# Row layout of tanh in a speech joint network: TensorE transposes with a PSUM copy, or SBUF-to-SBUF DMA transposes

## The chip, the cores and the metric

The kernel runs on one core of a Trainium2 chip. The metric is the device time of one execution in microseconds. A profiled execution also has a span, from its first to its last recorded instruction. The core has five engines with instruction queues of their own: TensorE (PE in the profile; PEld is its weight load), VectorE (DVE), ScalarE (ACT), GpSimd (POOL) and SyncE (SP), which here only issues DMAs.

## The reference

The forward pass is a small convolutional encoder and a joint network, and the reference returns its output and the gradients of all seven inputs. Cut to what matters:

```python
# x (2, 16000, 256), g (2, 8, 256); w1, w2 (3, 256, 256); w_f, w_g, w_o (256, 256), all bfloat16
h  = gelu(conv(x, w1))[:, ::2, :]            # three taps, then every second row: 8000 rows
f  = gelu(conv(h, w2))[:, ::2, :]            # 4000 rows
fe = einsum("btd,de->bte", f, w_f)
ge = einsum("bud,de->bue", g, w_g)
j  = tanh(fe[:, :, None, :] + ge[:, None, :, :])   # (2, 4000, 8, 256)
out = einsum("btud,dv->btuv", j, w_o)
# returned: out and the gradients of x, w1, w2, g, w_f, w_g, w_o for a given grad_out (2, 4000, 8, 256)
```

The product that the change touches is the gradient of w_o ("gwo"): the sum over b, t and u of j[b,t,u,d] * grad_out[b,t,u,v]. It contracts over t, so TensorE needs j with t on the partitions ("row layout"). The other uses of j, the output product and the derivative 1 - j*j, need or have d on the partitions ("column layout").

## The kernel before, in words

The 4000 rows of each of the two batches are cut into nine chunks: seven of 512 rows, one of 256 and one of 160, 18 chunks in all. For a chunk there are three stages, written as generators: stage_a (lines 243 to 293) computes the encoder up to FE and the row layouts HRo, HRe and FR; stage_j (331 to 401) is the joint network with its gradients; stage_de (438 to 552) is the rest of the backward pass, down to the gradients of x and of the encoder's weights. The main loop (626 to 649) runs them staggered: in iteration k it takes stage_j of chunk k, stage_a of chunk k+1 and stage_de of chunk k-1 in turns, in 16 steps. The scheduler of the language places the instructions on the engines' queues from this order and from the dependencies; on each queue they then run in order.

In stage_j the eight values of u are taken as four pairs (`up`), each of four steps. A step is one (j, dt): j is which u of the pair, dt which half of the 256 columns. Each step holds:

- gj (line 349): the product of WOT and GOT, the transposed gradient, into one of three PSUM buffers `psj`, from which line 357 makes NGZ and its sum on VectorE;
- in even steps, the row layout of tanh for two blocks of 128 rows (lines 363 to 380): up to eight TensorE transposes of JT into a `psj` buffer, and one VectorE copy into JR (three buffers);
- the output product of one block of 128 rows (387), copied by ScalarE into OUT (line 190 through line 389), which POOL's queue stores (398, 401);
- in odd steps, the gwo products (313) of a pair of blocks that was copied earlier; they add up in one PSUM bank, GWO_ps, over the whole kernel;
- one of the four tanh instructions (300) for the next pair: JT, with four buffers.

At the start of a pair, GOT (column layout of grad_out, DMA transposes from HBM on SP's queue, line 120) and GO (the same in row layout, POOL's queue, lines 129 and 134) are loaded two pairs ahead, with three buffers each. stage_a loads x for the next chunk as four DMA transposes XC (lines 108 and 112, seven buffers), also on SP's queue. The pool `keep` (line 71) gives HRo, HRe, FR, G1e, G1o and G2 three buffers each; the row layouts are made by to_rows (194) with TensorE, and read by the weight products of stage_de (lines 510 to 516) two iterations later. Before the main loop (lines 561 to 580) stage_a of chunk 0 is run, with the loads of WOT and the first GOT after the first piece of it, and the first tanh pair. At the end gg_out (598) uses two JR buffers for small tiles.

Of the kernel before, what the change touches and what calls it, by code (L numbers as in the profile page):

```python
# [10 lines left out]
BF16 = mybir.dt.bfloat16  # L11
# [10 lines left out]
def kernel(  # L22
# [19 lines left out]
    nc = tc.nc  # L42
    B, T, D = x.shape
    KK = w1.shape[0]
    U = g.shape[1]
    V = w_o.shape[1]
# [3 lines left out]
    KT = 2  # L50
    P = 128
# [22 lines left out]
    jtp = ctx.enter_context(tc.tile_pool(name="jtp", bufs=4))  # L74
    gop = ctx.enter_context(tc.tile_pool(name="gop", bufs=3))
    jop = ctx.enter_context(tc.tile_pool(name="jop", bufs=2))
    jrp = ctx.enter_context(tc.tile_pool(name="jrp", bufs=3))
    jzp = ctx.enter_context(tc.tile_pool(name="jzp", bufs=4))
    dep = ctx.enter_context(tc.tile_pool(name="dep", bufs=1))
    dep2 = ctx.enter_context(tc.tile_pool(name="dep2", bufs=2))  # L80
# [162 lines left out]
    def stage_a(g_):  # L243
        b, ci, c0, W = chunks[g_]
        S = st[g_]
        XC = xc_tiles.pop(g_)
        if g_ + 1 < NG:
            xc_tiles[g_ + 1] = load_xc(g_ + 1)
        HTe = htp.tile([P, KT, CW], BF16, name="HTe")
        HTo = htp.tile([P, KT, 2 + CW], BF16, name="HTo")  # L250
        G1e = keep.tile([P, KT, CW], BF16, name="G1e")
        G1o = keep.tile([P, KT, 2 + CW], BF16, name="G1o")
        if ci == 0:
            nc.gpsimd.memset(HTo[:, :, 0:2], 0.0)
            nc.gpsimd.memset(G1o[:, :, 0:2], 0.0)
        else:
            pv = st[g_ - 1]
            pw = chunks[g_ - 1][3]
            nc.gpsimd.tensor_copy(out=HTo[:, :, 1:2], in_=pv["HTo"][:, :, pw + 1:pw + 2])
            nc.gpsimd.tensor_copy(out=G1o[:, :, 1:2], in_=pv["G1o"][:, :, pw + 1:pw + 2])  # L260
        S["HTo"], S["G1e"], S["G1o"] = HTo, G1e, G1o
        mm_o = [(W1[:, i, kt], XC[c][:, kt, 16:16 + W]) for i, c in ((0, 1), (1, 2), (2, 3)) for kt in range(KT)]
        yield from conv_gelu(W, mm_o, HTo[:, :, 2:2 + W], G1o[:, :, 2:2 + W])
        mm_e = [(W1[:, i, kt], XC[c][:, kt, 16 + sh:16 + sh + W])
                for i, c, sh in ((0, 3, -1), (1, 0, 0), (2, 1, 0)) for kt in range(KT)]
        yield from conv_gelu(W, mm_e, HTe[:, :, 0:W], G1e[:, :, 0:W], ps_j if g_ == 0 else None)
        last = c0 + W == MQ
        FT = htp.tile([P, KT, CW], BF16, name="FT")
        G2 = keep.tile([P, KT, CW], BF16, name="G2")
        S["G2"] = G2  # L270
        mm_f = [(W2[:, i, kt], SRC[:, kt, off:off + W])
                for i, SRC, off in ((0, HTo, 1), (2, HTo, 2), (1, HTe, 0)) for kt in range(KT)]
        yield from conv_gelu(W, mm_f, FT[:, :, 0:W], G2[:, :, 0:W])
        S["FE"] = []
        for mt in range(KT):
            ps = ps_a()
            for kt in range(KT):
                nc.tensor.matmul(ps[:, :W], lhsT=WF[:, kt, mt * P:(mt + 1) * P], rhs=FT[:, kt, :W],  # L278
                                 start=(kt == 0), stop=(kt == KT - 1))
            FE = fep.tile([P, CW], FP32, name=f"FE{mt}")  # L280
            evac(FE[:, :W], ps[:, :W], "dve")
            S["FE"].append(FE)
        yield
        HRo = keep.tile([P, NB, D], BF16, name="HRo")
        HRe = keep.tile([P, NB, D], BF16, name="HRe")
        FR = keep.tile([P, NB, D], BF16, name="FR")
        S["HRo"], S["HRe"], S["FR"] = HRo, HRe, FR
        to_rows(HRo, HTo, 1, W + 1 if last else W)
        yield
        to_rows(HRe, HTe, 0, W)  # L290
        yield
        to_rows(FR, FT, 0, W)
        yield

    def tanh_pair(g_, up):
        b, ci, c0, W = chunks[g_]
        JT = jtp.tile([P, 2, KT, CW], BF16, name="JT")
        for j in range(2):
            for mt in range(KT):
                nc.scalar.activation(out=JT[:, j, mt, :W], in_=st[g_]["FE"][mt][:, :W], func=ACT.Tanh,  # L300
                                     bias=GE[:, b, mt, 2 * up + j:2 * up + j + 1], scale=1.0)
                yield JT

    nblk = [[(tb, min(P, W - tb * P)) for tb in range((W + P - 1) // P)] for (_, _, _, W) in chunks]
    n_gwo = sum(len(nb) for nb in nblk) * U * KT
    gwo_cnt = [0]

    def emit_gwo(g_, JR, GO, tbs):
        for tb, m in tbs:
            for j in range(2):  # L310
                for dt in range(KT):
                    n = gwo_cnt[0]
                    nc.tensor.matmul(GWO_ps[:, dt, :], lhsT=JR[:m, tb % 2, j, dt * P:(dt + 1) * P], rhs=GO[:m, tb, j, :],  # L313
                                     start=(n == 0), stop=(n == n_gwo - 1))
                    gwo_cnt[0] = n + 1

    pend_sum, pend_gwo = [], []

# [12 lines left out]
    def stage_j(g_):  # L331
# [1 line left out]
        b, ci, c0, W = chunks[g_]  # L333
        S = st[g_]
        for up in range(UP):
            JT, GOT, GO = S["JT"].pop(up), S["GOT"].pop(up), S["GO"].pop(up)
            ng, nup = (g_, up + 2) if up + 2 < UP else (g_ + 1, up + 2 - UP)
            if ng < NG:
                st[ng].setdefault("GOT", {})[nup] = load_got(ng, nup)
# [4 lines left out]
            for step in range(4):  # L344
# [15 lines left out]
                pend_sum.append((g_, u, dt, NGZ))  # L360
                if len(pend_sum) > 2:
                    emit_sum(*pend_sum.pop(0))
                if step % 2 == 0:
                    tbs = [t_ for t_ in nblk[g_] if t_[0] // 2 == step // 2]
                    if tbs:
                        tr = ps_j(BF16)
                        for tb, m in tbs:
                            for jj in range(2):
                                for kt in range(KT):
                                    o = (((tb % 2) * 2 + jj) * KT + kt) * P  # L370
                                    nc.tensor.transpose(out=tr[:m, o:o + P], in_=JT[:, jj, kt, tb * P:tb * P + m],  # L371
                                                        identity=ident[:])
                        JR = jrp.tile([P, 2, 2, D], BF16, name="JR")
                        ms = [m for _, m in tbs]
                        if len(set(ms)) == 1:
                            evac(JR[:ms[0], 0:len(ms)].rearrange("p a u d -> p (a u d)"), tr[:ms[0], 0:len(ms) * 512], "dve")
                        else:
                            for tb, m in tbs:
                                evac(JR[:m, tb % 2].rearrange("p u d -> p (u d)"), tr[:m, (tb % 2) * 512:(tb % 2 + 1) * 512], "dve")
                        pend_gwo.append((g_, JR, GO, tbs))  # L380
                for tb, m in nblk[g_]:
                    if tb != step:
                        continue
# [3 lines left out]
                            nc.tensor.matmul(ps[:m, jj * V:(jj + 1) * V], lhsT=JT[:, jj, kt, tb * P:tb * P + m],  # L387
                                             rhs=WO[:, kt, :], start=(kt == 0), stop=(kt == KT - 1))
                    evac(OUT[:m, tb].rearrange("p u v -> p (u v)"), ps[:m, :], "act")
                if step % 2 == 1 and len(pend_gwo) > 1:  # L390
                    emit_gwo(*pend_gwo.pop(0))
                if tgen is not None:
                    st[tg].setdefault("JT", {})[tup] = next(tgen)
                yield
# [163 lines left out]
    nc.scalar.activation(out=warm_[:, 1, 0:8], in_=warm[:, 0:8], func=ACT.Gelu_apprx_tanh)  # L558
    for _ in range(20):
        nc.tensor.matmul(warm_ps[:, 0:2 * P], lhsT=warm[:, 0:P], rhs=warm, start=True, stop=True)  # L560
    gen = stage_a(0)
    next(gen)
    first_mm, conv_o = marks[0], marks[5]
    nc.sync.dma_start_transpose(out=WOT[:], in_=w_o[:, :])
    st[0]["GOT"], st[0]["GO"] = {0: load_got(0, 0)}, {0: load_gor(0, 0)}
    next(gen)
    next(gen)
    next(gen)
# [29 lines left out]
    def gg_out():  # L598
# [4 lines left out]
        for b in range(B):  # L603
            nparts = sum(1 for c in chunks if c[0] == b)
            nc.vector.tensor_reduce(out=NGGE_all[:, b], in_=NGGE_parts[:, b, :, :, 0:nparts],
                                    axis=mybir.AxisListType.X, op=ALU.add)
            ngge_bf = accp.tile([P, KT, U], BF16, name=f"ngge_bf{b}")
            nc.vector.tensor_copy(out=ngge_bf[:], in_=NGGE_all[:, b])
            gg_ps = ps_j()
            for kt in range(KT):  # L610
                nc.tensor.matmul(gg_ps[:U, :D], lhsT=ngge_bf[:, kt, :], rhs=WGT[:, kt, :],
                                 start=(kt == 0), stop=(kt == KT - 1))
            gg_sb = jrp.tile([P, 2, 2, D], BF16, name="JR")
            nc.scalar.activation(out=gg_sb[:U, 0, 0], in_=gg_ps[:U, :D], func=ACT.Copy, scale=-1.0)
            nc.sync.dma_start(out=out_4[b], in_=gg_sb[:U, 0, 0])
            tr_ps = ps_j(BF16)
            for kt in range(KT):
                nc.tensor.transpose(out=tr_ps[:U, kt * P:(kt + 1) * P], in_=ngge_bf[:, kt, :], identity=ident[:])
            ngge_R = jrp.tile([P, 2, 2, D], BF16, name="JR")
            nc.vector.tensor_copy(out=ngge_R[:U, 0, 0], in_=tr_ps[:U, 0:D])  # L620
            for dt in range(KT):
                nc.tensor.matmul(GWG_ps[:, dt * D:(dt + 1) * D], lhsT=GR8[:, b, dt * P:(dt + 1) * P],
                                 rhs=ngge_R[:U, 0, 0], start=(b == 0 and dt == 0), stop=(b == B - 1 and dt == KT - 1))
# [56 lines left out]
```

## Time and profile before

| | |
|---|---|
| time, median of three runs | 1020.64 us (1013.41 to 1022.01) |
| profiled execution | 1007.04 us, its span 1005.3 us |
| TensorE clock granted in it | 0.988 of full, mean |
| DMA | 156.58 MB, mean 156 GB/s |

Each group of instructions is shown as line, engine, operation, output and inputs, shape and count; then the busy time, the mean time of one, and how long the engine had been idle before them and for whom. Some of the groups beside those of the change:

```profile
L190 ACT CAST OUT_SB<-psj 128x512 bf16<-128x512 f32 (+1 forms) x256 | 150.3, 587 | 165.4 <-PE psj L387 161.2
L357 DVE SCALAR_TENSOR_TENSOR NGZ<-JSQ,psj 128x512 bf16<-128x512 bf16 (+2 forms) x288 | 174.2, 611 | 55.3 <-PE psj L349 54.9
L349 PE MATMUL psj<-GOT,WOT 128*128 128x512 bf16 (+2 forms) x576 | 158.0, 351 | 7.8 <-DMA GOT<-in_grad_out_dram 6.6
...
L313 PE MATMUL GWO_ps<-GO_R,JR 128*128 128x256 bf16 (+1 forms) x1024 | 140.6, 273 | 0.0
```

Records of TensorE overlap[...]: a mean of 273 ns is not the distance from one to the next. The DMA queue q0 carries what POOL issues, q1 what SP issues.

### The profile page before, as it was taken

To read this page: it belongs to the slowest core of one execution; us is meant where nothing else is said; L and a number is where in the kernel's file an instruction comes from. 1 tells how busy PE (TensorE), PEld (TensorE's weight loads), DVE (VectorE), ACT (ScalarE), POOL (GpSimd) and SP (SyncE) were. 2 spreads that over 40 slices of the span, in tenths; PEclk is the share of its full clock that TensorE was granted. 3 is DMA by queue.
4 is the path that set the end of the run, shared out by engine and by line. 5 is a ranking of instruction groups with operands and counts; after the bars stand their busy time and mean duration, and the time that the engine had idled before them with its cause. 6 is when DMAs were issued, how large, how long until landed. Compare 5 with 4: busy or idle time off the path is not lost.

```text
span 1005.3 us, 20283 instructions
## 1 busy us (share of the span) xinstructions
PE 966.8 (96%) x8060; PEld 696.6 (69%) x8060; DVE 780.4 (78%) x1733; ACT 558.6 (56%) x983; POOL 211.3 (21%) x402
## 2 busy tenths in 40 slices
PE   5899999999999999999999999999999999999997
PEld 4567676776767668785765676676867767787873
DVE  3988886959778696868787885958879597877673
ACT  3966674655556464535755664636656455554522
POOL 2122112121111213123231112121121211212230
PEclk7999999999999999999999999999999999999997
DMA  8998848569473774947473847749484684836232
GB/s 168 178 219 207 191 126 180 145 179 196 137 179 107 147 192 148 172 138 197 120 187 103 192 112 179 162 127 220 130 197 110 162 175 130 170 119 168 93 109 61
DMA packets 237919, 156.58 MB, mean 156 GB/s; under 512 B 209504, under 2 KB 213632, under 8 KB 237824
## 3 DMA queue, kind: packets, MB, share of 16 engines
q0 software_dynamic: 29152, 102.69, 34.2%
q1 hardware_dynamic: 206800, 51.68, 31.4%
q8 instruction: 63, 1.03, 0.4%
q10 hardware_dynamic: 1872, 0.92, 0.3%
q14 instruction: 32, 0.26, 0.1%
HBM read 54.44 MB, written 50.34 MB: 104 GB/s over the span
## 4 chain that ended last, share of the span: by engine, by line
PE 80%; ACT 7%; DMA 6%; DVE 5%; SPq 1%; issue 1%; ACTq 0%; DVEq 0%; POOLq 0%
PE psa L502 14%; PE GWO_ps L313 10%; PE psj L387 9%; PE psa L233 9%; PE psj L349 9%; PE psa L533 7%; PE psab L199 6%; PE psjb L371 5%; DMA out_dram<-GX_SB 5%; PE psa L476 3%; ACT JT L300 2%; ACT g_s L216 1%; PE psa L482 1%; DMA GOT<-in_grad_out_dram 1%; ACT OUT_SB L190 1%; PE psa L278 1%
## 5 line engine op out<-in xcount | busy, mean ns | idle before, releaser
L190 ACT CAST OUT_SB<-psj 128x512 bf16<-128x512 f32 (+1 forms) x256 | 150.3, 587 | 165.4 <-PE psj L387 161.2
L357 DVE SCALAR_TENSOR_TENSOR NGZ<-JSQ,psj 128x512 bf16<-128x512 bf16 (+2 forms) x288 | 174.2, 611 | 55.3 <-PE psj L349 54.9
L349 PE MATMUL psj<-GOT,WOT 128*128 128x512 bf16 (+2 forms) x576 | 158.0, 351 | 7.8 <-DMA GOT<-in_grad_out_dram 6.6
L387 PE MATMUL psj<-WO,JT 128*128 128x256 bf16 (+1 forms) x1024 | 162.6, 273 | 0.2
L313 PE MATMUL GWO_ps<-GO_R,JR 128*128 128x256 bf16 (+1 forms) x1024 | 140.6, 273 | 0.0
L210 ACT ACTIVATE g_sq<-psa 128x512 bf16<-128x512 f32 (+2 forms) x106 | 57.7, 544 | 125.1 <-PE psa L233 122.7
L387 PEld LDWEIGHTS <-JT 128*128 128x128 bf16 (+1 forms) x1024 | 93.7, 98 | 38.5 <-issue 3.2
L313 PEld LDWEIGHTS <-JR 128*128 128x128 bf16 (+1 forms) x1024 | 98.5, 98 | 19.2 <-issue 2.3
L129 POOL DMA_DIRECT2D GO_R<-in_grad_out_dram x72 | 52.8, 734 | 268.5 <-PE GWO_ps L313 174.7
L192 DVE COPY JR<-psjb 128x1024 bf16<-128x1024 bf16 (+2 forms) x136 | 88.4, 653 | 10.7 <-PE psjb L371 10.7
L233 PE MATMUL psa<-XC,W_120 128*128 128x512 bf16 (+2 forms) x420 | 92.4, 353 | 1.3 <-DMA XC<-in_x_dram 1.2
L398 POOL DMA_DIRECT2D out_dram<-OUT_SB x72 | 53.4, 742 | 177.8 <-ACT OUT_SB L190 143.3
L355 DVE TENSOR_TENSOR JSQ<-JT 128x1024 bf16<-128x1024 bf16 (+2 forms) x144 | 87.3, 615 | 2.4
L371 PEld LDWEIGHTS <-JT 128*128 128x128 bf16 (+1 forms) x1024 | 69.9, 98 | 27.3 <-issue 0.9
L371 PE MATMUL psjb<-ident,JT 128*128 128x128 bf16 (+1 forms) x1024 | 88.0, 219 | 0.0
L192 DVE CAST GX_SB<-psa 128x512 bf16<-128x512 f32 x64 | 44.2, 691 | 45.0 <-PE psa L533 33.6
L436 DVE TENSOR_TENSOR ACC_GW_148<-ACC_GW_148,psa 128x512 f32<-128x512 f32 x48 | 33.0, 688 | 57.5 <-PE psa L502 57.5
L190 ACT CAST GX_SB<-psa 128x512 bf16<-128x512 f32 x64 | 37.4, 585 | 71.3 <-DMA out_dram<-GX_SB 37.1
L533 PE MATMUL psa<-W1T,GHo 128*128 128x256 bf16 (+1 forms) x384 | 74.1, 275 | 1.2 <-ACT GX_SB L190 1.0
L212 DVE SCALAR_TENSOR_TENSOR g_s<-g_sq,psa 128x512 bf16<-128x512 bf16 (+2 forms) x106 | 65.1, 614 | 12.2 <-ACT HTo L211 11.1
L349 PEld LDWEIGHTS <-WOT 128*128 128x128 bf16 x576 | 54.8, 98 | 28.4 <-DMA WOT<-in_w_o_dram 5.8
L533 PE MATMUL psa<-W1T,GHe 128*128 128x256 bf16 (+1 forms) x384 | 74.0, 275 | 0.1
(616 smaller groups left out, 1886.5 us busy)
## 6 DMA issues: line engine op xcount, KB each, us to landing
GO_R<-in_grad_out_dram POOLq DMA_DIRECT2D x56, 512.0 KB, 4.6
out_dram<-OUT_SB POOLq DMA_DIRECT2D x56, 512.0 KB, 5.4
out_dram<-GX_SB POOLq DMA_DIRECT2D x60, 256.0 KB, 3.2
GOT<-in_grad_out_dram SPq DMA_TRANSPOSE x144, 5.4
GO_R<-in_grad_out_dram POOLq DMA_DIRECT2D x8, 256.0 KB, 4.4
out_dram<-OUT_SB POOLq DMA_DIRECT2D x8, 256.0 KB, 4.5
XC<-in_x_dram SPq DMA_TRANSPOSE x72, 4.7
out_dram<-g_sq SPq DMA_DIRECT2D x9, 128.0 KB, 1.9
```

What stands on the lines that cost most here:

```text
L190: nc.scalar.copy(out=out, in_=in_)
L192: nc.vector.tensor_copy(out=out, in_=in_)
L212: nc.vector.scalar_tensor_tensor(out=th, in0=sq, scalar=1.0, in1=ps, op0=ALU.add, op1=ALU.mult)
L233: mm = nc.tensor.matmul(ps[:, :W], lhsT=w[:, mt * P:(mt + 1) * P], rhs=rhs, start=(k == 0), stop=(k == len(mms) - 1))
L313: nc.tensor.matmul(GWO_ps[:, dt, :], lhsT=JR[:m, tb % 2, j, dt * P:(dt + 1) * P], rhs=GO[:m, tb, j, :], start=(n == 0), stop=(n == n_gwo - 1))
L349: mm = nc.tensor.matmul(gj[:, :W], lhsT=WOT[:, kt, dt * P:(dt + 1) * P], rhs=GOT[:, j, kt, :W], start=(kt == 0), stop=(kt == KT - 1))
L355: nc.vector.tensor_tensor(out=JSQ[:, :, :W], in0=JT[:, j, :, :W], in1=JT[:, j, :, :W], op=ALU.mult)
L357: nc.vector.scalar_tensor_tensor(out=NGZ[:, :W], in0=JSQ[:, dt, :W], scalar=1.0, in1=gj[:, :W], op0=ALU.subtract, op1=ALU.mult, accum_out= ...
L371: nc.tensor.transpose(out=tr[:m, o:o + P], in_=JT[:, jj, kt, tb * P:tb * P + m], identity=ident[:])
L387: nc.tensor.matmul(ps[:m, jj * V:(jj + 1) * V], lhsT=JT[:, jj, kt, tb * P:tb * P + m], rhs=WO[:, kt, :], start=(kt == 0), stop=(kt == KT - 1))
L502: nc.tensor.matmul(ps[:, dt * D:(dt + 1) * D], lhsT=lhs(bl, m, dt), rhs=rhs[:m, bl, :], start=(k == 0), stop=(k == n - 1))
L533: nc.tensor.matmul(ps[:m, cj * D:(cj + 1) * D], lhsT=l_, rhs=r_, start=(k == 0), stop=(k == len(mms) - 1))
```

## The change

tanh_pair, which makes JT for the next pair, now also makes JR, in row layout, for all its blocks: JR is one tile of 2 x 2 x 4 blocks of 128 columns, with two buffers in place of three smaller ones. After the second tanh of a j, SP issues DMA transposes from JT in SBUF to JR in SBUF: one for a chunk of 512 rows, and one for each half of d in the smaller chunks. A chunk of 160 rows is filled up to 256 columns with zeros by POOL first. The TensorE transposes and the VectorE copies of the row layout are gone. The gwo products are taken per j over all blocks of the chunk: those of j = 0 are put on the list in step 2 and emitted in step 3, those of j = 1 in step 3 and emitted in step 0 of the next pair. HRo, HRe and FR move to a pool with two buffers. The loads of WOT, of the first GOT and of the first GO are placed before stage_a of chunk 0, and so before the loads of XC for chunk 1. gg_out takes its two small tiles from OUT's buffers.

```diff
--- before.py
+++ after.py
@@ -74,7 +74,8 @@
     jtp = ctx.enter_context(tc.tile_pool(name="jtp", bufs=4))
     gop = ctx.enter_context(tc.tile_pool(name="gop", bufs=3))
     jop = ctx.enter_context(tc.tile_pool(name="jop", bufs=2))
-    jrp = ctx.enter_context(tc.tile_pool(name="jrp", bufs=3))
+    jrp = ctx.enter_context(tc.tile_pool(name="jrp", bufs=2))
+    keep2 = ctx.enter_context(tc.tile_pool(name="keep2", bufs=2))
     jzp = ctx.enter_context(tc.tile_pool(name="jzp", bufs=4))
     dep = ctx.enter_context(tc.tile_pool(name="dep", bufs=1))
     dep2 = ctx.enter_context(tc.tile_pool(name="dep2", bufs=2))
@@ -281,9 +282,9 @@
             evac(FE[:, :W], ps[:, :W], "dve")
             S["FE"].append(FE)
         yield
-        HRo = keep.tile([P, NB, D], BF16, name="HRo")
-        HRe = keep.tile([P, NB, D], BF16, name="HRe")
-        FR = keep.tile([P, NB, D], BF16, name="FR")
+        HRo = keep2.tile([P, NB, D], BF16, name="HRo")
+        HRe = keep2.tile([P, NB, D], BF16, name="HRe")
+        FR = keep2.tile([P, NB, D], BF16, name="FR")
         S["HRo"], S["HRe"], S["FR"] = HRo, HRe, FR
         to_rows(HRo, HTo, 1, W + 1 if last else W)
         yield
@@ -295,24 +296,34 @@
     def tanh_pair(g_, up):
         b, ci, c0, W = chunks[g_]
         JT = jtp.tile([P, 2, KT, CW], BF16, name="JT")
+        JR = jrp.tile([P, 2, KT, NB, P], BF16, name="JR")
+        Wp = (W + P - 1) // P * P
         for j in range(2):
             for mt in range(KT):
                 nc.scalar.activation(out=JT[:, j, mt, :W], in_=st[g_]["FE"][mt][:, :W], func=ACT.Tanh,
                                      bias=GE[:, b, mt, 2 * up + j:2 * up + j + 1], scale=1.0)
-                yield JT
+                if mt == KT - 1:
+                    for dt in range(KT):
+                        if Wp > W:
+                            nc.gpsimd.memset(JT[:, j, dt, W:Wp], 0.0)
+                        if Wp < CW:
+                            nc.sync.dma_start_transpose(out=JR[:, j, dt, 0:Wp // P, :], in_=JT[:, j, dt, :Wp])
+                    if Wp == CW:
+                        nc.sync.dma_start_transpose(out=JR[:, j].rearrange("p k t d -> p (k t) d"),
+                                                    in_=JT[:, j].rearrange("p k t -> p (k t)"))
+                yield JT, JR
 
     nblk = [[(tb, min(P, W - tb * P)) for tb in range((W + P - 1) // P)] for (_, _, _, W) in chunks]
     n_gwo = sum(len(nb) for nb in nblk) * U * KT
     gwo_cnt = [0]
 
-    def emit_gwo(g_, JR, GO, tbs):
-        for tb, m in tbs:
-            for j in range(2):
-                for dt in range(KT):
-                    n = gwo_cnt[0]
-                    nc.tensor.matmul(GWO_ps[:, dt, :], lhsT=JR[:m, tb % 2, j, dt * P:(dt + 1) * P], rhs=GO[:m, tb, j, :],
-                                     start=(n == 0), stop=(n == n_gwo - 1))
-                    gwo_cnt[0] = n + 1
+    def emit_gwo(g_, JR, GO, j):
+        for tb, m in nblk[g_]:
+            for dt in range(KT):
+                n = gwo_cnt[0]
+                nc.tensor.matmul(GWO_ps[:, dt, :], lhsT=JR[:m, j, dt, tb, :], rhs=GO[:m, tb, j, :],
+                                 start=(n == 0), stop=(n == n_gwo - 1))
+                gwo_cnt[0] = n + 1
 
     pend_sum, pend_gwo = [], []
 
@@ -333,7 +344,7 @@
         b, ci, c0, W = chunks[g_]
         S = st[g_]
         for up in range(UP):
-            JT, GOT, GO = S["JT"].pop(up), S["GOT"].pop(up), S["GO"].pop(up)
+            (JT, JR), GOT, GO = S["JT"].pop(up), S["GOT"].pop(up), S["GO"].pop(up)
             ng, nup = (g_, up + 2) if up + 2 < UP else (g_ + 1, up + 2 - UP)
             if ng < NG:
                 st[ng].setdefault("GOT", {})[nup] = load_got(ng, nup)
@@ -360,24 +371,6 @@
                 pend_sum.append((g_, u, dt, NGZ))
                 if len(pend_sum) > 2:
                     emit_sum(*pend_sum.pop(0))
-                if step % 2 == 0:
-                    tbs = [t_ for t_ in nblk[g_] if t_[0] // 2 == step // 2]
-                    if tbs:
-                        tr = ps_j(BF16)
-                        for tb, m in tbs:
-                            for jj in range(2):
-                                for kt in range(KT):
-                                    o = (((tb % 2) * 2 + jj) * KT + kt) * P
-                                    nc.tensor.transpose(out=tr[:m, o:o + P], in_=JT[:, jj, kt, tb * P:tb * P + m],
-                                                        identity=ident[:])
-                        JR = jrp.tile([P, 2, 2, D], BF16, name="JR")
-                        ms = [m for _, m in tbs]
-                        if len(set(ms)) == 1:
-                            evac(JR[:ms[0], 0:len(ms)].rearrange("p a u d -> p (a u d)"), tr[:ms[0], 0:len(ms) * 512], "dve")
-                        else:
-                            for tb, m in tbs:
-                                evac(JR[:m, tb % 2].rearrange("p u d -> p (u d)"), tr[:m, (tb % 2) * 512:(tb % 2 + 1) * 512], "dve")
-                        pend_gwo.append((g_, JR, GO, tbs))
                 for tb, m in nblk[g_]:
                     if tb != step:
                         continue
@@ -387,8 +380,10 @@
                             nc.tensor.matmul(ps[:m, jj * V:(jj + 1) * V], lhsT=JT[:, jj, kt, tb * P:tb * P + m],
                                              rhs=WO[:, kt, :], start=(kt == 0), stop=(kt == KT - 1))
                     evac(OUT[:m, tb].rearrange("p u v -> p (u v)"), ps[:m, :], "act")
-                if step % 2 == 1 and len(pend_gwo) > 1:
+                if pend_gwo:
                     emit_gwo(*pend_gwo.pop(0))
+                if step >= 2:
+                    pend_gwo.append((g_, JR, GO, step - 2))
                 if tgen is not None:
                     st[tg].setdefault("JT", {})[tup] = next(tgen)
                 yield
@@ -558,11 +553,11 @@
     nc.scalar.activation(out=warm_[:, 1, 0:8], in_=warm[:, 0:8], func=ACT.Gelu_apprx_tanh)
     for _ in range(20):
         nc.tensor.matmul(warm_ps[:, 0:2 * P], lhsT=warm[:, 0:P], rhs=warm, start=True, stop=True)
+    nc.sync.dma_start_transpose(out=WOT[:], in_=w_o[:, :])
+    st[0]["GOT"], st[0]["GO"] = {0: load_got(0, 0)}, {0: load_gor(0, 0)}
     gen = stage_a(0)
     next(gen)
     first_mm, conv_o = marks[0], marks[5]
-    nc.sync.dma_start_transpose(out=WOT[:], in_=w_o[:, :])
-    st[0]["GOT"], st[0]["GO"] = {0: load_got(0, 0)}, {0: load_gor(0, 0)}
     next(gen)
     next(gen)
     next(gen)
@@ -610,13 +605,13 @@
             for kt in range(KT):
                 nc.tensor.matmul(gg_ps[:U, :D], lhsT=ngge_bf[:, kt, :], rhs=WGT[:, kt, :],
                                  start=(kt == 0), stop=(kt == KT - 1))
-            gg_sb = jrp.tile([P, 2, 2, D], BF16, name="JR")
+            gg_sb = jop.tile([P, NB, 2, V], BF16, name="OUT_SB")
             nc.scalar.activation(out=gg_sb[:U, 0, 0], in_=gg_ps[:U, :D], func=ACT.Copy, scale=-1.0)
             nc.sync.dma_start(out=out_4[b], in_=gg_sb[:U, 0, 0])
             tr_ps = ps_j(BF16)
             for kt in range(KT):
                 nc.tensor.transpose(out=tr_ps[:U, kt * P:(kt + 1) * P], in_=ngge_bf[:, kt, :], identity=ident[:])
-            ngge_R = jrp.tile([P, 2, 2, D], BF16, name="JR")
+            ngge_R = jop.tile([P, NB, 2, V], BF16, name="OUT_SB")
             nc.vector.tensor_copy(out=ngge_R[:U, 0, 0], in_=tr_ps[:U, 0:D])
             for dt in range(KT):
                 nc.tensor.matmul(GWG_ps[:, dt * D:(dt + 1) * D], lhsT=GR8[:, b, dt * P:(dt + 1) * P],
```

## The prediction

> **What bounds the kernel now.** I read the page's busy shares first, then the chain that ended last, then the groups of the lines that change, then the DMA queues, and last what the SP queue, which will issue the new transposes, waits for.
>
> ```profile
> span 1005.3 us, 20283 instructions
> ...
> PE 966.8 (96%) x8060; PEld 696.6 (69%) x8060; DVE 780.4 (78%) x1733; ACT 558.6 (56%) x983; POOL 211.3 (21%) x402
> ...
> q0 software_dynamic: 29152, 102.69, 34.2%
> q1 hardware_dynamic: 206800, 51.68, 31.4%
> ...
> PE 80%; ACT 7%; DMA 6%; DVE 5%; SPq 1%; issue 1%; ACTq 0%; DVEq 0%; POOLq 0%
> ```
>
> TensorE carries 80% of the chain. Between 100 and 960 us it was busy 843.75 of 860 us, so in the long middle it idled 16 us in all: whatever leaves TensorE there shortens the kernel, until something else fills up. The DMA engines are 66% busy (the sum of all five queues), VectorE 78%.
>
> ```profile
> L192 DVE COPY JR<-psjb 128x1024 bf16<-128x1024 bf16 (+2 forms) x136 | 88.4, 653 | 10.7 <-PE psjb L371 10.7
> ...
> L371 PE MATMUL psjb<-ident,JT 128*128 128x128 bf16 (+1 forms) x1024 | 88.0, 219 | 0.0
> ...
> GOT<-in_grad_out_dram SPq DMA_TRANSPOSE x144, 5.4
> ```
>
> These are what goes (1024 TensorE transposes and 136 VectorE copies) and the nearest thing to what comes: a DMA transpose of the same 256 KB, but from HBM. The 88.0 us of L371 counts overlapping records; the chain has eight of them in 0.45 us, again and again, 56 ns each.
>
> ```profile
> SPq L120 <- PE psj L387: 460.5, 44, 15.8
> SPq L112 <- PE psj L349: 51.7, 13, 11.2
> ```
>
> The SP queue spends most of its time waiting for a GOT or XC buffer to be freed by TensorE. It has slack; the question is how much of it the change uses.
>
> [...] the 144 GOT transposes take 1.292 us of SP in the median, and loads of 160 rows (two in 2.47 us) take nearly as long as those of 512 (two in 2.57), so there is no price per tile from HBM[...]. [...] Here q1's packets took 31.4% of 16 x 1005.3 us / 206,800 = 24.4 ns each for 250 bytes, which is 164 GB/s over 16 engines[...].
>
> **The change part by part.**
> 1. TensorE transposes: -1024 x 56 ns = -57 us, all on the path. Bounds -50 (the 5% of L371 in the chain) to -60.
> 2. VectorE copies: -88 us of VectorE, off the path (VectorE waits 10.7 us for exactly these). Their PSUM buffers go too, out of the three that gj and OUT share; TensorE waited 1.1 us for those. Worth 0 to -3; I take 0, TensorE's own work hiding it.
> 3. The gwo matmuls stay 1024 in number. They come per j instead of per pair of blocks, in step 3 and in step 0 of the next pair, so GO_R is freed no later. 0; TensorE streams them alike.
> 4. SP's new work: 14 chunks of 512 x 4 pairs x 2 = 112 transposes of 64 tiles, and 4 small chunks x 4 x 2 x 2 = 64 of 16 tiles. SP has 225 transposes now x 1.29 = 290 us. With t the price per tile on top of the 1.29: 290 + 176 x 1.29 + (112 x 64 + 64 x 16) t = 517 us + 8192 t. The trace shows no transpose from SBUF, so t is bounded: 0 if it behaves as from HBM (517 us, half the span)[...]. Then SP's work no longer fits into the time that TensorE needs. SP is in order: behind a JR transpose stand the GOT load two pairs ahead and the next chunk's four XC loads, and TensorE waits for all three kinds. The last GOT load now goes out at 958.5 us, 47 us before the end; that tail stays. 1050 + 47 = 1097 us span.
> 5. DMA engines: 112 x 1024 + 64 x 256 = 131,072 packets x 24.4 ns / 16 = +200 us, 20 points. A full chunk takes 60.0 us (250.45 to 310.47) with a share of 0.65, so 39 us of work, +12.5: 51.5 of the 56.4 us that would be left after step 1. It fits, tightly; bounds 0 (hidden) to +62 us (rival two).
> 6. The new wait: JR's transpose waits for ScalarE's tanh on the SP queue. JR is used five or six steps of 3.75 us (a sixteenth of a chunk) later, some 20 us, against a landing of 5.4 us; 0 while SP keeps up. With two JR buffers the older one is read for the last time in step 0, before the first new transpose in step 1.
> 7. Memsets for W = 160: 32 on POOL, at 0.19 to 0.52 us (its nearest rows) 6 to 17 us of an engine that is 21% busy; 0 on the path, or a few us if they stand behind a blocked store.
> 8. keep2 with two buffers: the row copies HRo, HRe and FR of a chunk wait for the weight products of two chunks before, emitted about a step later. TensorE has the pair's work in between; 0, at most 18 x 1 us.
> 9. WOT and the first GOT before XC of chunk 1: now SP issues WOT at 11.58 after seven XC loads, and TensorE waits 5.75 us for GOT at 21.1. Three issues earlier: -4, bounds 0 (the DMA engines are full there, share 1.04 from 25 to 50 us) to -6. gg_sb and ngge_R in OUT_SB's buffers: 0, at the end when those are free.
>
> Without step 4: 1005.3 - 57 - 4 = 944. With it, SP's 1097 is the larger and sets the end. The profiled execution lay 1.7 us above its span (1007.04) and 13.6 below the runs' median (1020.64); I add half of the spread to 1099 and forecast **1105 us**.
>
> **The rivals.** One, faster: t is so small that SP keeps up. Its own formula decides: 517 + 8192 t + 47 is below 1005 for t under 54 ns. For it speaks that HBM transposes have no price per tile[...]. TensorE then bounds at 944, and the fuller DMA engines give back some 12 us, because stores of GX_SB already hold ScalarE for 37.1 us over 14 times. 956 span, 965 by the runs. Two, slower without SP: packets read from SBUF cost more on the engines. Above 24.4 x (56.4 - 39) / 12.5 = 34 ns the engines no longer fit into a chunk; at twice the price, 49 ns, a chunk needs 64 us, +4 x 15.6 chunks = +62, 1067 span, some 1075 by the runs. For it: share above 1 between 50 and 80 us already. [...] Three, no change: gain and contention cancel, -61 by steps 1 and 9 and +61 by waits for GOT, XC and GX_SB: 1005 span, 1015 by the runs. That the change is not what it says (transposes still on TensorE) is excluded by the diff: L371 is deleted.
>
> **How the numbers follow.** SP as the bound has 0.48: 1050 to 1240, with 0.11 beyond that for a costlier tile. Rival one 0.32 (945 to 1000), rival two 0.12, rival three 0.08. The predicted time is that of the SP case, whose own range is 1050 to 1240. Both signs hold much, so the range reaches from 948 to 1240; outside are 0.11 above and some 0.05 below. About 1% is what a measurement of this kernel can tell from no change. Faster 0.32, same 0.08, slower 0.60.
>
> **What would show it.** SP transposes of JR at 5 us or more each with JT and GOT waits vanishing from SP's list (it never waits), and TensorE waiting for DMA of JR, GOT or XC: step 4 right. JR issues at 1.3 to 3 us, TensorE still above 95% and L371 gone: rival one. DMA share near 1 throughout with SP waiting: rival two. [...]

## The result, and the profile after

The changed kernel takes 1053.68 us (median of four runs, 1049.53 to 1062.14), the kernel before 1017.02 us in runs beside it: a ratio of 1.0368 with a 95% interval of 1.0281 to 1.0456, slower. The profiled execution took 1052.29 us, its span is 1050.5. Below, a ratio is always against the kernel before, measured on the same chip with that experiment, and one point is a hundredth of its time, some 10.2 us. A time is the median of all runs of a kernel, but its ratio leaves out runs that lie a few per cent above the rest, so the two can differ a little.

The page of the changed kernel, in the order of the prediction: busy shares, 25 or 26 us slices, DMA queues, then the groups around JR.

```profile
span 1050.5 us, 18601 instructions
...
PE 945.3 (90%) x7036; PEld 643.1 (61%) x7036; DVE 704.3 (67%) x1597; ACT 561.0 (53%) x983; POOL 215.5 (21%) x434
...
PE   7349699999989899897789999998989999899997
...
DMA  8579999796989969897977968996979899698542
...
q1 hardware_dynamic: 343504, 85.26, 52.0%
q0 software_dynamic: 29152, 102.69, 35.6%
...
L324 PE MATMUL GWO_ps<-GO_R,JR 128*128 128x256 bf16 (+1 forms) x1024 | 157.8, 277 | 49.3 <-DMA JR<-JT 49.3
```

TensorE went from 96% busy to 90%; VectorE lost 76 us. The first slices of TensorE's row, 7 3 4 9 6, are new: TensorE is idle for long near the start. The group of the gwo products has a wait that it did not have, 49.3 us for JR's DMA. The DMA engines are now 88.5% busy, against 66%.

The transposes that fill JR, on SP's queue (shortest, median and longest in ns), and first, for comparison, the loads of GOT from HBM in the kernel before:

```profile
L120 SPq DMA_TRANSPOSE GOT<-in_grad_out_dram x144: 1173/1292/6408, 14.2 to 958.5; - x144
...
L312 SPq DMA_TRANSPOSE JR<-JT x112: 1231/1508/7967, 73.6 to 938.9; - x112
L310 SPq DMA_TRANSPOSE JR<-JT x64: 1167/1195/1952, 39.2 to 1015.8; - x64
```

This alone refutes the price on which the forecast stood: a transpose of 64 tiles (L312; the prediction counts in tiles of 16 x 128 elements) took SP at least 1.23 us, one of 16 tiles (L310) at least 1.17. The difference of 48 tiles is worth 1 ns a tile by the shortest and 7 ns by the medians. The 1050 us that the forecast gave SP mean t = 65 ns in its formula; that was the author's assumption, which no trace had shown. SP's queue, though in use for 735 us by the sum of its 401 transposes' records, still waits:

```profile
SPq L121 <- PE psj L380: 152.1, 22, 18.5
SPq L312 <- ACT OUT_SB L191: 65.4, 26, 7.9
```

So why is the kernel slower at all? Two stretches, windows of the kernel before and of the changed one (busy time of each engine, granted clock, DMA share):

```profile
25.00:50.00 25.00, 21.47 (x165) 14.11 (x164) 23.03 (x61) 22.96 (x45) 3.77 (x7) 1.00 1.04 177
50.00:100.00 50.00, 48.70 (x405) 34.83 (x403) 45.01 (x104) 34.53 (x58) 12.54 (x23) 1.00 1.00 212
```

```profile
25.00:50.00 25.00, 8.27 (x43) 4.62 (x41) 7.09 (x18) 6.47 (x15) 1.34 (x3) 0.66 0.56 115
50.00:100.00 50.00, 33.96 (x212) 20.65 (x211) 29.44 (x76) 29.02 (x52) 9.18 (x15) 0.80 0.86 165
```

Between 25 and 100 us TensorE was busy for 70 us before and for 42 us after. To place the loss I took when VectorE's NGZ instruction of each chunk's first step begins. Chunk 1 begins at 55.2 us before and at 85.4 after, chunk 2 at 103.8 and 141.5: 38 us late. The last NGZ is 45 us late. **The start loses 38 us, and the other 16 chunks, which should have won some 50, lose 7 more.** There are two things to explain.

The timelines of the changed kernel show the first: SP's queue, then TensorE.

```profile
19.55 6.25 SPq L121 DMA_TRANSPOSE GOT<-in_grad_out_dram  x4
25.91 2.58 SPq L113 DMA_TRANSPOSE XC<-in_x_dram  x2
28.58 1.33 SPq L109 DMA_TRANSPOSE XC<-in_x_dram  x1
29.96 1.25 SPq L631 DMA_TRANSPOSE WFT<-in_w_f_dram  x1
31.27 3.87 SPq L631 DMA_TRANSPOSE W2T<-in_w_dram  x3
35.18 3.88 SPq L631 DMA_TRANSPOSE W1T<-in_w_dram  x3
39.16 7.63 SPq L310 DMA_TRANSPOSE JR<-JT  x6
```

```profile
25.38 0.27 PE L336 MATMUL sum_470<-NGZ,ident 128*128 128x256 bf16 x1
41.53 0.39 PE L324 MATMUL GWO_ps<-GO_R,JR 128*128 128x256 bf16 x1 [15.88 <-DMA JR<-JT]
```

The first pair's tanh began at 18.24 us and TensorE wanted JR after 25.65, but SP first issued fourteen transposes that are needed later, end to end and 1.23 us or more each; TensorE stood still for 15.88 us. TensorE's own waits, over the whole execution, name another pair as well:

```profile
PE GWO_ps L324 <- DMA JR<-JT: 49.3, 14, 15.9
PE psa L528 <- DVE GX_SB L193: 24.7, 10, 4.2
```

Of the first wait, 32.3 us fall before 110 us and 17.0 after it. The second was much smaller before (10.6 us for all copies into GX_SB): the products of stage_de wait for GX_SB's copy, and that copy for an earlier store of the same buffer. Before, then after:

```profile
ACT GX_SB L190 <- DMA out_dram<-GX_SB: 37.1, 14, 4.8
DVE GX_SB L192 <- DMA out_dram<-GX_SB: 11.2, 8, 2.3
```

```profile
DVE GX_SB L193 <- DMA out_dram<-GX_SB: 42.7, 15, 5.3
ACT GX_SB L191 <- DMA out_dram<-GX_SB: 39.2, 19, 3.7
```

### The profile page after: what moved, and what is told of

It is laid out like the page before. It is cut to its first block, busy times and chain, and to the rows that moved or that the text cites. A ratio compares the mean times of both kernels' runs of the same rounds, so it can differ in the third digit from the quotient of the medians.

```text
span 1050.5 us, 18601 instructions
## 1 busy us (share of the span) xinstructions
PE 945.3 (90%) x7036; PEld 643.1 (61%) x7036; DVE 704.3 (67%) x1597; ACT 561.0 (53%) x983; POOL 215.5 (21%) x434
## 3 DMA queue, kind: packets, MB, share of 16 engines
q1 hardware_dynamic: 343504, 85.26, 52.0%
## 5 line engine op out<-in xcount | busy, mean ns | idle before, releaser
L368 DVE SCALAR_TENSOR_TENSOR NGZ<-JSQ,psj 128x512 bf16<-128x512 bf16 (+2 forms) x288 | 173.4, 611 | 55.2 <-PE psj L360 54.4
L324 PE MATMUL GWO_ps<-GO_R,JR 128*128 128x256 bf16 (+1 forms) x1024 | 157.8, 277 | 49.3 <-DMA JR<-JT 49.3
L380 PE MATMUL psj<-WO,JT 128*128 128x256 bf16 (+1 forms) x1024 | 175.3, 275 | 0.3 <-ACT JT L303 0.2
L360 PE MATMUL psj<-GOT,WOT 128*128 128x512 bf16 (+2 forms) x576 | 162.0, 356 | 0.3
L380 PEld LDWEIGHTS <-JT 128*128 128x128 bf16 (+1 forms) x1024 | 98.9, 99 | 63.7 <-issue 3.0
L234 PE MATMUL psa<-XC,W_123 128*128 128x512 bf16 (+2 forms) x420 | 94.8, 363 | 0.0
L528 PEld LDWEIGHTS <-GHo 128*128 128x128 bf16 (+1 forms) x384 | 37.7, 99 | 43.5 <-issue 37.6
L538 POOL DMA_DIRECT2D out_dram<-GX_SB x64 | 35.3, 552 | 137.4 <-ACT GX_SB L191 78.3
L234 PEld LDWEIGHTS <-W_123 128*128 128x128 bf16 x432 | 42.0, 100 | 33.7 <-issue 5.9
```

The lines of the kernel that those rows point to most:

```text
L234: mm = nc.tensor.matmul(ps[:, :W], lhsT=w[:, mt * P:(mt + 1) * P], rhs=rhs, start=(k == 0), stop=(k == len(mms) - 1))
L324: nc.tensor.matmul(GWO_ps[:, dt, :], lhsT=JR[:m, j, dt, tb, :], rhs=GO[:m, tb, j, :], start=(n == 0), stop=(n == n_gwo - 1))
L360: mm = nc.tensor.matmul(gj[:, :W], lhsT=WOT[:, kt, dt * P:(dt + 1) * P], rhs=GOT[:, j, kt, :W], start=(kt == 0), stop=(kt == KT - 1))
L368: nc.vector.scalar_tensor_tensor(out=NGZ[:, :W], in0=JSQ[:, dt, :W], scalar=1.0, in1=gj[:, :W], op0=ALU.subtract, op1=ALU.mult, accum_out= ...
L528: nc.tensor.matmul(ps[:m, cj * D:(cj + 1) * D], lhsT=l_, rhs=r_, start=(k == 0), stop=(k == len(mms) - 1))
```

## The experiments

Theory S: the loss comes from SP's queue and the waits for JR behind it. Theory D: from the load on the DMA engines, which makes everything else land later. Theory R: from another part of the change. The diffs show what matters, with some names shortened. Several readings below rest on when chunks 2 and 17 begin, in one profiled execution each:

| us | chunk 2 begins | from there to chunk 17 | from there to the end |
|---|---|---|---|
| kernel before | 103.8 | 850.2 | 51.3 |
| e1, no JR transposes | 100.1 | 794.5 | 61.9 |
| e2, transposes without a reader | 132.9 | 815.6 | 62.9 |
| e8, as e2, four GX_SB buffers | 135.8 | 790.7 | 61.7 |
| changed kernel | 141.5 | 846.1 | 62.9 |

**No row layout (e1).** The gwo products read JT in its own layout, so gwo itself is not computed.

```diff
-   nc.sync.dma_start_transpose(out=JR..., in_=JT...)
-   nc.tensor.matmul(GWO_ps[:, dt, :], lhsT=JR[:m, j, dt, tb, :], ...)
+   nc.tensor.matmul(GWO_ps[:, dt, :], lhsT=JT[:m, j, dt, tb * P:(tb + 1) * P], ...)
```

> The changed kernel without any row layout of tanh: no JR transposes, and the gwo products read JT in its column layout (their number and shapes stay; gwo itself is not computed). It shows what the change would bring if the new DMAs cost nothing. Three theories. S: the loss of the change is made on SP's queue, above all at the start, where JR's transposes stand behind loads that are needed later, and TensorE waits for them. D: the loss is made on the DMA engines, which the new transposes fill to 88%, so that everything else lands later. R: something else of the change costs (two buffers for HRo, HRe and FR, the new order of the gwo products). S and D: 940 to 955 us by the runs. R: above 975 us.

Measured: 960.01 us, ratio 0.9449 (0.9375 to 0.9523), a little above the stated 940 to 955 and well below R's 975. The change without its DMAs brings 5.5 points. Two buffers for the rows and the new order of the products, which e1 contains, cost little: 5 us are missing against the upper end of the stated range.

**The transposes, without a reader (e2).** The same, with the JR transposes kept; gwo is again not computed.

```diff
    nc.sync.dma_start_transpose(out=JR..., in_=JT...)
-   nc.tensor.matmul(GWO_ps[:, dt, :], lhsT=JR[:m, j, dt, tb, :], ...)
+   nc.tensor.matmul(GWO_ps[:, dt, :], lhsT=JT[:m, j, dt, tb * P:(tb + 1) * P], ...)
```

> The changed kernel with all JR transposes issued, but the gwo products read JT instead of JR (gwo is not computed), so nobody waits for JR and the load on SP and the DMA engines stays. S: the waits for JR are gone, 955 to 975 us. D: the load alone costs, 1005 to 1045 us.

Measured: 1017.83 us, ratio 0.9987 (0.9950 to 1.0023). The load alone costs 5.4 points, which is the whole gain; the wait for JR on top of it makes 3.8 more (1.0368 - 0.9987). That is D's number, but e2 keeps the transposes on SP's queue too, so it can't tell SP's load from that of the DMA engines. By the table, 33 of the load's 55 us are lost before chunk 2 begins; of the 39 us that the wait for JR adds, 9 are lost there and 30 later.

**Another order at the start (e3).**

```diff
+   # SP: the four JR transposes of the first pair first
+   after(got_0_1, first_jr, sync=False)
+   after(xc_2, first_jr, sync=False); after(got_0_2, first_jr, sync=False)
+   after(weight_transpose, first_jr, sync=False)
```

> The changed kernel with SP's order at the start changed alone: the four transposes of JR for the first pair go before the second GOT, the later GOTs of chunk 0, XC of chunk 2 and the seven weight transposes. S: the 15.9 us wait and part of the others of the first two chunks go, 1015 to 1030 us. D: 1045 to 1055 us, since the DMAs are the same.

Measured: 1047.31 us, ratio 1.0262 (1.0172 to 1.0351). The expected 1015 to 1030 was missed; the interval overlaps that of the changed kernel. JR's first four transposes now went out at 20.80 us, against 39.16 in the changed kernel, yet the waits for JR stayed:

```profile
PE GWO_ps L337 <- DMA JR<-JT: 49.7, 13, 10.5
```

The longest fell from 15.9 to 10.5 us, and others took its place. S in this form falls: it is not one bad position. From this comes S2: at the start SP has no time left, and each transpose more costs its 1.25 us. For it speaks the stretch from 25 to 50 us of the changed kernel, where 20 issues fill 23.5 us of SP's queue while the DMA engines' share is 0.56. The fill of SP's queue over the first 100 us, 90.3 us by its records against 85.0 in the kernel before, shows nothing by itself: in e1, without one JR transpose, it is 96.0, and chunk 2 begins earlier than in the kernel before. SP's records were longer where the DMA engines were full (in the changed kernel 1.27 us in the mean where the share during the record was under 0.6, 2.10 where it was over 0.95).

**Four GX_SB buffers (e5).**

```diff
-   gxp = ctx.enter_context(tc.tile_pool(name="gxp", bufs=2))
+   gxp = ctx.enter_context(tc.tile_pool(name="gxp", bufs=4))
```

> The changed kernel with four GX_SB buffers in place of two. D: the stores of GX_SB, late because the DMA engines are full, no longer hold VectorE, ScalarE and TensorE in the middle: 1015 to 1030 us. S: 1045 to 1055 us.

Measured: 1018.48 us, ratio 0.9883 (0.9779 to 0.9986). D's number, and the transposes are all still there. The four runs reach from 1002.30 to 1039.63 us, further apart than those of any other kernel here, so the size of the gain is uncertain: 3.6 points by the medians, 4.9 by the ratios. Either way it is the largest single repair.

**Chunk 0 on TensorE (e7).**

```diff
-   if Wp < CW:
+   if Wp < CW and g_ > 0:
        nc.sync.dma_start_transpose(out=JR..., in_=JT...)
+   if g_ == 0:
+       nc.tensor.transpose(out=tr[:, o:o + P], in_=JT[:, j, dt, tb * P:(tb + 1) * P], identity=ident[:])
+       ...
+       evac(JR[:, j, :, 0:Wp // P, :], tr..., "dve")
```

> The changed kernel with the row layout of chunk 0 alone made by TensorE and VectorE again (all other chunks by DMA): 16 of the 176 JR transposes leave SP's queue, with 2% of the bytes. S2, the theory left of S: in the first 100 us SP issues without a break at 1.25 us a transpose whatever its size, so each one more there delays the start by its 1.25 us: -15 to -30 us against the changed kernel, 1022 to 1040 us. D: 2% of the bytes are nothing, 1048 to 1056 us.

Measured: 1030.18 us, ratio 1.0123 (1.0085 to 1.0161), 2.45 points better than the changed kernel, as S2 said. The packets that went were 4,608 of 136,704, some 3.4% (the expectation said 2%). The edit also takes away every wait for JR in chunk 0, so alone it doesn't tell SP's issue time from late landings; the next run does that better.

**Half as many transposes in the small chunks, the same bytes (e9).**

```diff
+   # chunks under 512 rows: JT and JR without gaps, one transpose for both halves of d
+   JT = JT[:].rearrange("p u k t -> p (u k t)")[:, 0:2 * KT * Wp].rearrange("p (u k t) -> p u k t", u=2, k=KT)
+   JR = JR[:].rearrange("p u k t d -> p (u k t d)")[:, 0:2 * KT * Wp].rearrange(...)
```

> The changed kernel with JT and JR of the chunks of 256 and 160 rows laid out without gaps, so that one transpose takes both halves of d: the same bytes in 32 transposes in place of 64, 8 in place of 16 in chunk 0. S2: 8 x 1.25 = 10 us of SP's time at the start are free, 1038 to 1047 us. D: the bytes count, not the instructions, 1050 to 1056 us.

Measured: 1046.10 us, ratio 1.0250 (1.0150 to 1.0349). The median is S2's, but the intervals overlap (1.0281 to 1.0456 for the changed kernel), so the ratio alone doesn't settle it. In the traces chunk 1 begins at 73.9 us instead of 85.4, 11.5 us earlier for eight instructions fewer, some 1.4 us each, with the same bytes.

**The early loads alone, in the kernel before (e4).**

```diff
+   nc.sync.dma_start_transpose(out=WOT[:], in_=w_o[:, :])
+   st[0]["GOT"], st[0]["GO"] = {0: load_got(0, 0)}, {0: load_gor(0, 0)}
    gen = stage_a(0)
    next(gen)
    ...
-   nc.sync.dma_start_transpose(out=WOT[:], in_=w_o[:, :])
-   st[0]["GOT"], st[0]["GO"] = {0: load_got(0, 0)}, {0: load_gor(0, 0)}
```

> The kernel before with the loads of WOT and of the first GOT and GO alone moved ahead of stage_a of chunk 0, as in the change. Both theories: TensorE's wait of 5.75 us for the first GOT goes, 1009 to 1017 us, unless SP, which issues without a break there, pays it back a little later: then 1017 to 1021 us.

Measured: 1019.71 us, ratio 1.0031 (1.0002 to 1.0061), the second alternative. Its trace has chunk 0 4.2 us early and chunk 1 5.3 us late: SP issues end to end over the first 45 us of it, and what is moved ahead there pushes something else back.

**Two row buffers and four GX_SB buffers in the kernel before (e6).**

```diff
+   keep2 = ctx.enter_context(tc.tile_pool(name="keep2", bufs=2))
-   HRo = keep.tile([P, NB, D], BF16, name="HRo")
+   HRo = keep2.tile([P, NB, D], BF16, name="HRo")
    ...
-   gxp = ctx.enter_context(tc.tile_pool(name="gxp", bufs=2))
+   gxp = ctx.enter_context(tc.tile_pool(name="gxp", bufs=4))
```

> The kernel before with two buffers for HRo, HRe and FR, as in the change, and four for GX_SB in the room that this frees. D: its DMA engines have slack and the stores of GX_SB hold TensorE for only 10.6 us, so the gain is small, 1005 to 1018 us, and most of what the four buffers give the changed kernel (36 us) is specific to it. If they give here as much as there (below 995 us), the loss in the middle isn't due to the transposes. If two buffers for the rows cost by themselves, above 1025 us.

Measured: 1005.20 us, ratio 0.9907 (0.9879 to 0.9934), at the lower end of D's range: 0.9 points, against 3.6 to 4.9 from the same four buffers in the changed kernel. The stalls on GX_SB existed before; the transposes multiplied them.

**The load without a reader, with four GX_SB buffers (e8).** e2 with e5's edit; gwo is not computed.

> The changed kernel with four GX_SB buffers, and the gwo products reading JT (gwo is not computed) while all JR transposes are still issued: the load of the transposes without the wait for them and without the wait for GX_SB's stores. With two buffers the load cost 58 us (1018 against 960). If the stores of GX_SB carry the load's cost in the middle: 980 to 995 us, and what is left is the start. If the DMA engines' fill costs in other ways too (GOT, XC, OUT_SB late): 1000 to 1015 us.

Measured: 982.79 us, ratio 0.9653 (0.9604 to 0.9701), 3.3 points better than e2. ScalarE's wait and TensorE's, in e2:

```profile
ACT GX_SB L191 <- DMA out_dram<-GX_SB: 55.0, 18, 5.4
...
PE psa L528 <- ACT GX_SB L191: 26.5, 13, 3.4
```

Neither row is left in e8, whose DMA engines are fuller than ever, 95.8% by the sum of its queues. From chunk 2 to chunk 17 it gains 59 us on the kernel before, and e1, without the transposes, 56. In the middle, then, GX_SB's buffers were the way in which the load cost anything without the wait for JR. What is left of the load in e8 is the start: chunk 2 begins 32 us late, in e1 3.7 us early.

**Both repairs (e10), chunk 1 as well (e12), half of the rest as well (e13).** They compute everything.

```diff
+   gxp = ... bufs=4
+   if g_ == 0:                  # e10: TensorE makes JR
+   if g_ < 2:                   # e12
+   if g_ < 2 or j == 1:         # e13
```

> The changed kernel with both repairs: chunk 0's row layout on TensorE, and four GX_SB buffers. If the two costs are separate, the gains add: 1054 - 23 - 36 = 995 us, 988 to 1003. If they are one and the same fill of the DMA engines, one repair takes the other's gain: 1010 to 1020 us.

Measured: 1002.39 us, ratio 0.9838 (0.9779 to 0.9896), in the stated 988 to 1003, near its upper end. By the ratios the two repairs bring 5.3 points together; 2.45 and e5's 3.6 to 4.9 would make 6.1 to 7.3. So they are separate in the main, and overlap in part.

> As the run before, with chunk 1's row layout on TensorE too, since TensorE there still waited 16.4 us for a JR transpose behind SP's full queue at about 100 us. S2: another -10 to -17 us, 975 to 990 us, below the kernel before with four GX_SB buffers (1005 us). If the late JR is a matter of any chunk, not of the start: within 5 us of the run before.

Measured: 997.08 us, ratio 0.9792 (0.9743 to 0.9841); 5 us better than e10 with overlapping intervals. S2's 975 to 990 was missed, and the other alternative, within 5 us of e10, is the nearer one. At the start S2 did hold in the trace: chunk 2 begins at 108.1 us, against 127.7 in e10. That trace is of the longest of the four runs (1010.17 us), so it can't show what became of these 20 us later; this stays open.

> As the run before, but from chunk 2 on only the row layout of j = 0 goes by DMA and that of j = 1 stays on TensorE: half the DMA load for half of TensorE's gain. If the waits of the middle grow faster than the load, this is the fastest version, 970 to 985 us; if not, the 25 us of TensorE's transposes come back, 990 to 1005 us.

Measured: 990.41 us, ratio 0.9750 (0.9699 to 0.9800), at the lower edge of the second expected range, 990 to 1005; yet, as the first alternative said, it has the lowest time of those that compute everything. Its interval overlaps e12's, but lies below that of e6 (0.9879 to 0.9934). The 76 of 176 transposes that are left fill the DMA engines to 80.8%, with TensorE 96% busy again; the waits for JR shrank to one:

```profile
PE psj L368 <- DMA GOT<-in_grad_out_dram: 6.4, 1, 6.4
PE GWO_ps L332 <- DMA JR<-JT: 5.9, 1, 5.9
```

## Why the prediction was wrong, step by step

The kernel got slower, as forecast, but 1105 us were forecast and 1053.68 measured, and the direction came out right by luck: with the price per tile as measured, the prediction's own formula gives SP some 570 to 620 us, and so the first rival, a faster kernel.

The step that failed is **step 4**, SP's work of 517 us + 8192 t, with an assumed t of 65 ns. Measured, t is 1 to 7 ns, and SP shows no price per tile from SBUF that matters, as it shows none from HBM (two loads of 160 rows took 2.47 us, two of 512 rows 2.57). The constant term was mis-sized too: 1.29 us is the median of an issue, but the mean in the kernel before is 374 / 225 = 1.66 us; issues took longer there where the DMA engines were full (1.26 us in the mean where the share during the issue was under 0.6, 1.98 where it was over 0.95). So it is with SP's sum of 735 us: the larger JR transposes took 2.21 us in the mean against 1.25 for the smaller, but 1.28 against 1.23 where the share was under 0.6 (12 and 23 of them), and XC's loads from HBM grew as well, from 1.55 to 2.05 us in the mean. These 735 us fit into the span. The idea that SP bounds holds for one place, the start, where its issues follow each other without a break from 25 to 50 us and where the 16 transposes of chunk 0 and the first of chunk 1 had to fit in. I summed SP over the kernel and did not look at it by stretch.

Step 5 took the DMA engines' fill at no cost because 51.5 us of work fit into 56.4. The work was about as forecast (q1's packets 25.4 ns against 24.4; its busy share times the span rose by 231 us, not 200), but the load's cost was 5.4 points (e1 to e2): some 33 us at the start, where SP's queue and the DMA engines both carry it, and some 21 from chunk 2 to chunk 17 through GX_SB, since they are gone in e8. Fitting on average says nothing about a store that must land before its buffer is used again, with two buffers. The 37.1 us that ScalarE already waited for those stores was the sign; I used it for 12 us in rival one.

Step 6 costed the wait for JR at 0 while SP keeps up. It cost 3.8 points (e2 to the changed kernel), 9 us at the start, where SP did not keep up, and 30 after it, although SP had time left on average. There TensorE waited six times for JR, 6.3 us at the longest, while JR's landings took up to 19.6 us, with a median of 5.2, where 5.4 had been assumed. Part of these 30 us belongs to both waits at once: with four GX_SB buffers the wait for JR costs 2.3 points by the ratios (e8 to e5).

Step 1 was right: with step 9 it promised 61 us, and e1 brought 5.5 points, 56 us. Steps 2 and 3 agree with e1, which contains them; the gwo products began 109 ns apart in the median, before the change and after it. Step 8 at nothing agrees with e1 and e6, which both have the two row buffers and are faster than the kernel before. Step 9 forecast -4 and brought +0.3 points (e4). Step 7's 32 memsets took POOL from 211.3 to 215.5 us; they were not tried by themselves, but e1 contains them.

Of the rivals, the first had the right price (t far below 54 ns) and the wrong end, since it allowed 12 us for contention where load and wait together took 9.2 points. The second named the engines' fill, by packets that cost 34 ns or more; they cost 25.4, and in e1, without a single one from SBUF, as much. That its 1075 us lie closest to the result is luck too. What SP's transposes cost the DMAs that POOL issues, e1 and e2 show: with the transposes, POOL's stores of GX_SB landed 3.4 us after their issue in the median instead of 2.3, and VectorE's wait for them rose from 13.3 to 35.2 us, ScalarE's from 37.8 to 55.0.

What stays open: at the start SP's issue time and the order of its queue cannot be fully told apart by ratios (e9's interval overlaps). That the DMA engines were not the limit there between 25 and 50 us, the window with a share of 0.56 shows; from 80 to 120 us their share is above 1 (1.05 to 1.23), and there they may be. Why JR comes late in the middle was not tried by itself either: SP's JR transposes of the full chunks waited 48.2 us for gwo products, which read the older of the two JR buffers, and 119.1 us for ScalarE, which makes JT, with the loads of GOT and XC behind them on the queue. A third JR buffer would have tested the first of these.

## What to carry to other kernels

Moving work from a full engine to the DMA engines brings that engine's time back only if each transfer that already had a deadline keeps it (here the load took 5.4 points of a gain of 5.5): look for stores whose buffers come round soon, and give them buffers before adding load. Sum a queue's issue time by stretch, above all at the start, since an issue here cost some 1.2 us or more, whether it moved 64 KB or 256. Moving half of the work may beat moving all of it: e13's median is the lowest of those that compute everything, though its interval overlaps those of e10 and e12.

## What the runs showed of the hardware

A DMA transpose from SBUF to SBUF cost the issuing queue as much as one from HBM (at least 1.17 us): at least 1.17 us for 128 x 256 elements and 1.23 us for 128 x 1024. The DMA engines took about as long per packet: q1's mean was 25.4 ns both in the changed kernel, with 136,704 of 343,504 packets from SBUF, and in e1, with none, against 24.4 in the kernel before. With a DMA share of 1.09 during it, one issue of the larger kind took SP 7.97 us. TensorE's granted clock was lower where it had to wait, 0.66 between 25 and 50 us, and 0.953 in the mean of the changed kernel against 0.988. A stall then cost more than its own time: the same six products took 1.46 us before the stall of 15.88 us, at a granted clock of 1.00, and 2.77 just after it, at 0.50.

```profile
22.08 1.46 PE L234 MATMUL psa<-XC,W_123 128*128 128x512 bf16 x6
...
43.40 2.77 PE L234 MATMUL psa<-XC,W_123 128*128 128x512 bf16 x6
```
